# VectorE's order of two instructions in a fused attention and rational-FFN kernel: the odd unit's numerator ahead of the next unit's mask

## The chip, the cores and the metric

The kernel runs on one core of a Trainium2 chip. The metric is the device time of one execution in microseconds. A core has five engines that run their own instruction streams in order and wait for each other by semaphores: TensorE (PE, with its weight loads shown as PEld), VectorE (DVE), ScalarE (ACT), GpSimd (POOL) and SyncE (SP, which issues the DMAs here). Matmul results lie in PSUM, all else in SBUF.

## The reference

Two layers: an attention through 32 inducing points, and an FFN whose activation is a rational function. The output of the first (4 batches of 12480 tokens, 128 wide) is the input of the second (hidden width 2048).

```python
h = mab(I, x)                 # 32 inducing points look at all 12480 tokens of a batch
attn_out = mab(x, h)          # each token looks at the 32 results
h = attn_out @ w_in           # 49920 x 128 by 128 x 2048
P = a[0] + a[1] * h + a[2] * h2 + a[3] * h3
Q = 1.0 + np.abs(b[0]) * np.abs(h) + np.abs(b[1]) * h2
g = P / (Q + 1e-06)
return (g @ w_out).astype(np.float32)
```

## The kernel before

A batch has 26 blocks of 480 tokens, a block has eight **units**, and a unit is 256 of the 2048 hidden columns: two matmuls into a PSUM tile `hp` of 128 x 960. There are 832 units. The attention of the coming blocks and batches, the reshaping of weights and the output copies are cut into small **side jobs**, which `side` (line 680) puts between the units' instructions when a budget allows.

`fast_ticks` (line 777) writes the order out by hand. In tick t it emits work for units of several ages. Units come in **pairs**, an even one and the odd one behind it, which share the two halves of one SBUF tile `u`. The rational function is written as a product of factors; the denominator comes from a logarithm and a sigmoid. By the names that the profile prints, a pair passes through:

- PE `hp<-at,st`: the matmuls of `first`. `hp` has three PSUM buffers, so a unit's matmul needs what read `hp` three units earlier to be done.
- DVE `u<-hp`: the **mask** of the even unit, which clears the sign bit: u = |h|.
- ACT `u<-hp,all`: the odd unit's **magnitude** (Abs with a bias).
- POOL `l<-u,all`: the even unit's **first factor**, from the mask's u.
- DVE `l<-hp,all,l`: the **even numerator**, from h and POOL's first factor.
- DVE `l<-u,all,hp`: the **odd numerator**, from h and ACT's magnitude.
- ACT `u<-u` over both halves (128 x 1920): the **logarithm**, in place over u; it needs the last reader of u, which is the odd numerator, to be done. Then ACT `u<-u,all`: the **sigmoid**. Four pairs make a group of eight ticks: four logarithms, a change of ACT's table, four sigmoids, a change back. The group's fourth logarithm is that of its youngest pair.
- DVE `l<-l,all,u`: the even unit's **last factor**, from l and the finished u, both in SBUF; ten or eleven ticks after its start.
- POOL `u<-l,all` and `l<-u`: the same for the odd unit in two instructions (`last_on_pool`, line 827). The first overwrites the even half of u, so it waits for VectorE's last factor.
- PE `po<-l,w_out`: the matmuls of `second`, summed over the block's eight units. Then DVE `oT<-po`, the **output copy**, once in a block (that is, once in four pairs), at the start of an even tick.

In an even tick VectorE gets mask and odd numerator, and POOL the first factor. In an odd tick VectorE gets last factor and even numerator, and POOL its two instructions. Side jobs follow in each tick. Every engine keeps the program's order (`keep_in_program_order`). All recorded instructions carry line 157, that of the recording helper, so the names and shapes tell them apart.

Of the kernel before, what the change touches and what calls it, by code (L numbers as in the profile page):

```python
# [14 lines left out]
ALU = mybir.AluOpType  # L15
# [157 lines left out]
class Kernel:  # L173
# [603 lines left out]
    def fast_ticks(self, units):  # L777

        V, A, G, p = self.nc.vector, self.nc.scalar, self.nc.gpsimd, self.params
        n = len(units)
        at = lambda t: units[t] if 0 <= t < n else None
        self.first(units[0])
        for t in range(n + 13):
            u, last, d = at(t), at(t - 1), at(t - 11)
            group, turn = divmod(t - 6, 8)
            w = at(8 * group + 2 * (turn % 4))
            late = at(t - 12) and at(t - 12).key[2] == 0  # L790
            if late:
                self.fetched = self.fetch()
            if at(t - 12) and not late:
                self.second(at(t - 12))
            if at(t + 1):
                self.first(at(t + 1))
            if t % 2:
                if d:
                    V.scalar_tensor_tensor(out=d.g, in0=d.g, scalar=p.k3, in1=d.u, op0=ALU.add, op1=ALU.mult)
                    self.last_on_pool(at(t - 10), d)  # L800
                if last:
                    V.scalar_tensor_tensor(out=last.g, in0=last.h, scalar=p.k2, in1=last.g, op0=ALU.add, op1=ALU.mult)
            else:
                if u:
                    u.pair = self.mp.tile([P, 2, 2, BT], F32, tag="u", name=f"u{u.i}", bufs=7)
                    u.u = u.pair[:, 0]
                    V.tensor_scalar(out=u.u.bitcast(I32), in0=u.h.bitcast(I32), scalar1=0x7FFFFFFF, scalar2=None, op0=ALU.bitwise_and)
                if last:
                    last.g = self.new(last, "l", 14)
                    V.scalar_tensor_tensor(out=last.g, in0=last.u, scalar=p.k1, in1=last.h, op0=ALU.add, op1=ALU.mult)  # L810
                if u:
                    u.g = self.new(u, "l", 14)
                    G.tensor_scalar(out=u.g, in0=u.u, scalar1=1.0, scalar2=p.k1, op0=ALU.mult, op1=ALU.add)
            self.run_act(turn == 4)
            if w and turn < 4:
                A.activation(w.pair, w.pair, AF.Ln, bias=LAM, scale=LAM)
            elif w:
                A.activation(w.pair, w.pair, AF.Sigmoid, bias=p.lnc, scale=-2.0)
            if u and t % 2:
                u.u = last.pair[:, 1]  # L820
                A.activation(u.u, u.h, AF.Abs, bias=p.back, scale=1.0)
            self.side(u or units[-1])
            if late:
                self.second(at(t - 12))
        self.fetch()
# [123 lines left out]
```

## Time and profile before

| | us |
|---|---|
| median of 3 runs | 2594.55 (2594.13 to 2599.68) |
| profiled execution | 2594.75 |
| its span (first to last instruction) | 2592.9 |
| mean granted TensorE clock in it | 0.966 of full |

Busy time is a sum over instructions and hides waits inside an instruction: where an instruction of one kind has two typical durations, the longer one holds a wait. The columns of the group rows are: line, engine, operation, output<-inputs, shapes, count, then busy time and mean ns of one, and the idle time of the engine just before them with what ended it. The POOL and ACT groups that matter here and that are not shown further down:

```profile
L157 POOL TENSOR_TENSOR l<-u 128x960 f32<-128x960 f32 x416 | 932.2, 2241 | 34.7
L157 POOL TENSOR_SCALAR u<-l,all 128x960 f32<-128x960 f32 x416 | 445.5, 1071 | 392.8 <-DVE l L157 363.4
L157 ACT ACTIVATE u<-u 128x1920 f32<-128x1920 f32 x416 | 739.8, 1799 | 193.2 <-DVE l L157 143.0
```

There are 416 of each, one a pair.

### The profile page before, as it was taken

What the parts mean: (1) busy time and instruction counts of PE and PEld (TensorE: products, weight loads), DVE (VectorE), ACT (ScalarE), POOL (GpSimd) and SP (SyncE); (2) the same over time, 40 slices, a digit from 0 to 9 for tenths busy, and PEclk for the clock granted to TensorE, in tenths of its full rate; (3) what the DMA queues carried; (4) which work ended last, traced back from release to release, by engine and by line L of the source; (5) the groups of instructions that cost most, each with busy time, mean ns of one, the idle gap of its engine ahead of it and who ended that gap; (6) DMA issues with size and microseconds to landing.
All of it is one profiled execution on the core that took longest, in us unless ns stands there. A gap on an engine that the chain in (4) does not pass through costs nothing.

```text
span 2592.9 us, 24006 instructions
## 1 busy us (share of the span) xinstructions
PE 2249.2 (87%) x7508; PEld 1233.8 (48%) x7508; DVE 2210.1 (85%) x2318; ACT 2244.9 (87%) x1590; POOL 2011.4 (78%) x1420
## 2 busy tenths in 40 slices
PE   7798888999899789989988898888888888888887
PEld 4544444555454355544544465444435434434333
DVE  6578778899899889899898888988889888888886
ACT  1488889989889999888899998899999999999996
POOL 2267767888787788888687887887888887888887
PEclk9699989999999999999999999999999999999999
DMA  7222201211222012112321131011101001000000
GB/s 251 73 62 78 73 27 52 71 50 31 70 83 80 19 31 76 50 48 63 92 55 48 35 88 38 16 42 31 46 27 50 27 20 38 20 22 24 17 17 17
DMA packets 117357, 133.68 MB, mean 52 GB/s; under 512 B 13544, under 2 KB 115816, under 8 KB 117224
## 3 DMA queue, kind: packets, MB, share of 16 engines
q1 hardware_dynamic: 117224, 132.06, 17.6%
q8 instruction: 64, 1.05, 0.2%
q14 instruction: 69, 0.57, 0.1%
HBM read 80.89 MB, written 25.56 MB: 41 GB/s over the span
## 4 chain that ended last, share of the span: by engine, by line
DVE 32%; PE 22%; ACT 19%; POOL 18%; issue 6%; DMA 1%; SPq 1%; DVEq 0%; POOLq 0%; ACTq 0%
DVE l L157 21%; ACT u L157 13%; POOL l L157 13%; PE po L157 13%; DVE u L157 7%; ACT L157 4%; POOL u L157 4%; PE hp L157 3%; PE ph L157 2%; PE pd L157 2%; DVE oT L157 1%; POOL a L157 1%; SPq L157 1%; DVE asm L157 1%; DMA x<-x_t 1%
## 5 line engine op out<-in xcount | busy, mean ns | idle before, releaser
L157 PE MATMUL po<-l,w_out 128*128 128x480 f32 x3328 | 1545.8, 592 | 188.4 <-POOL l L157 183.6
L157 PEld LDWEIGHTS po<-l,w_out 128*128 128x128 f32 x3328 | 607.3, 194 | 773.0 <-issue 419.7
L157 POOL TENSOR_TENSOR l<-u 128x960 f32<-128x960 f32 x416 | 932.2, 2241 | 34.7
L157 ACT ACTIVATE u<-u 128x1920 f32<-128x1920 f32 x416 | 739.8, 1799 | 193.2 <-DVE l L157 143.0
L157 PE MATMUL hp<-at,st 128*128 128x480 f32 x1664 | 742.7, 529 | 98.3 <-DVE l L157 91.1
L157 ACT ACTIVATE u<-u,all 128x1920 f32<-128x1920 f32 x416 | 766.1, 1887 | 1.2
L157 POOL TENSOR_SCALAR u<-l,all 128x960 f32<-128x960 f32 x416 | 445.5, 1071 | 392.8 <-DVE l L157 363.4
L157 DVE SCALAR_TENSOR_TENSOR l<-l,all,u 128x960 f32<-128x960 f32 x416 | 597.8, 1437 | 105.7 <-ACT u L157 105.3
L157 DVE SCALAR_TENSOR_TENSOR l<-hp,all,l 128x960 f32<-128x960 f32 x416 | 503.5, 1210 | 121.8 <-POOL l L157 114.0
L157 POOL TENSOR_SCALAR l<-u,all 128x960 f32<-128x960 f32 x416 | 555.6, 1336 | 64.7 <-DVE u L157 63.7
L157 DVE TENSOR_SCALAR u<-hp 128x960 int32<-128x960 int32 x416 | 477.0, 1147 | 75.6 <-PE hp L157 74.3
L157 PEld LDWEIGHTS hp<-at,st 128*128 128x128 f32 x1664 | 312.6, 193 | 431.3 <-issue 325.3
L157 DVE SCALAR_TENSOR_TENSOR l<-u,all,hp 128x960 f32<-128x960 f32 x416 | 500.3, 1203 | 0.3 <-ACT u L157 0.3
L157 ACT ACTIVATE u<-hp,all 128x960 f32<-128x960 f32 x416 | 434.7, 1045 | 36.4 <-PE hp L157 36.3
L157 ACT ACT_TABLE_LOAD x234 | 300.2, 1283 | 4.9 <-PEq L942 0.7
L157 PE MATMUL ph<-x,eT 120*32 120x129 f32 x832 | 105.8, 280 | 9.0 <-DMA x<-x_t 6.3
L157 PEld LDWEIGHTS pd<-HT,xTb 128*120 128x120 f32 x832 | 103.3, 198 | 9.7 <-DMA xTb<-x_c 4.3
L157 PE MATMUL pd<-HT,xTb 128*120 128x32 f32 x832 | 100.5, 277 | 5.2 <-DMA xTb<-x_c 4.1
L157 PEld LDWEIGHTS ph<-x,eT 120*32 120x32 f32 x832 | 88.9, 112 | 28.0 <-issue 21.5
L157 DVE COPY oT<-po 128x480 f32<-128x480 f32 x104 | 67.3, 647 | 21.6 <-PE po L157 21.3
L157 PE MATMUL po<-at,st 128*128 128x480 f32 x104 | 80.7, 776 | 0.0
L157 PE MATMUL pc<-xTa,ind 128*128 128x480 f32 x156 | 72.2, 566 | 1.9 <-DMA xTa<-x_c 1.9
(84 smaller groups left out, 621.6 us busy)
## 6 DMA issues: line engine op xcount, KB each, us to landing
x<-x_t SPq DMA_DIRECT2D x104, 240.0 KB, 3.5
xTb<-x_c SPq DMA_DIRECT2D x104, 240.0 KB, 2.8
at<-hl SPq DMA_DIRECT2D x416, 60.0 KB, 2.0
out<-oT SPq DMA_DIRECT2D x104, 240.0 KB, 2.0
xTa<-x_c SPq DMA_DIRECT2D x78, 240.0 KB, 2.8
xTw<-x_c SPq DMA_DIRECT2D x5, 960.0 KB, 10.3
raw<-w_in SPq DMA_DIRECT2D x4, 480.0 KB, 14.2
raw<-w_out SPq DMA_DIRECT2D x5, 384.0 KB, 5.9
```

What stands on the lines that cost most here:

```text
L157: ins = call(*args, **kw)
```

## The change

In an even tick VectorE's two instructions change places: the odd numerator of the unit before comes first, then the mask of the even unit.

```diff
             else:
+                if last:
+                    last.g = self.new(last, "l", 14)
+                    V.scalar_tensor_tensor(out=last.g, in0=last.u, scalar=p.k1, in1=last.h, op0=ALU.add, op1=ALU.mult)
                 if u:
                     u.pair = self.mp.tile([P, 2, 2, BT], F32, tag="u", name=f"u{u.i}", bufs=7)
                     u.u = u.pair[:, 0]
                     V.tensor_scalar(out=u.u.bitcast(I32), in0=u.h.bitcast(I32), scalar1=0x7FFFFFFF, scalar2=None, op0=ALU.bitwise_and)
-                if last:
-                    last.g = self.new(last, "l", 14)
-                    V.scalar_tensor_tensor(out=last.g, in0=last.u, scalar=p.k1, in1=last.h, op0=ALU.add, op1=ALU.mult)
                 if u:
                     u.g = self.new(u, "l", 14)
                     G.tensor_scalar(out=u.g, in0=u.u, scalar1=1.0, scalar2=p.k1, op0=ALU.mult, op1=ALU.add)
```

VectorE's order before, in the last batch (a name such as `u3_20_6` is the tile u of batch 3, block 20, unit 6; the number behind it counts tiles):

```order
L157 TENSOR_SCALAR u3_20_6_13187<-hp3_20_6_13173 128x960
L157 SCALAR_TENSOR_TENSOR l3_20_5_13189<-u3_20_4_13161,all_193,hp3_20_5_13158 128x960
L157 SCALAR_TENSOR_TENSOR l3_19_4_13068<-l3_19_4_13068,all_193,u3_19_4_13064 128x960
L157 SCALAR_TENSOR_TENSOR l3_20_6_13191<-hp3_20_6_13173,all_193,l3_20_6_13191 128x960
L157 TENSOR_SCALAR u3_21_0_13210<-hp3_21_0_13196 128x960
L157 SCALAR_TENSOR_TENSOR l3_20_7_13212<-u3_20_6_13187,all_193,hp3_20_7_13184 128x960
```

The same place in VectorE's order after the change:

```order
L157 SCALAR_TENSOR_TENSOR l3_20_5_13187<-u3_20_4_13163,all_193,hp3_20_5_13158 128x960
L157 TENSOR_SCALAR u3_20_6_13189<-hp3_20_6_13173 128x960
L157 SCALAR_TENSOR_TENSOR l3_19_4_13068<-l3_19_4_13068,all_193,u3_19_4_13066 128x960
L157 SCALAR_TENSOR_TENSOR l3_20_6_13191<-hp3_20_6_13173,all_193,l3_20_6_13191 128x960
L157 SCALAR_TENSOR_TENSOR l3_20_7_13210<-u3_20_6_13189,all_193,hp3_20_7_13184 128x960
L157 TENSOR_SCALAR u3_21_0_13212<-hp3_21_0_13196 128x960
```

Of each pair the odd numerator (`l3_20_5`, `l3_20_7`) moved ahead of the mask (`u3_20_6`, `u3_21_0`); last factor and even numerator kept their places. The last factor now stands directly behind the mask.

ScalarE's order around the fourth logarithm of the group that ends with `u3_20_6`, after the change; it is the same before, but for the tiles' numbers:

```order
L157 ACTIVATE u3_20_4_13163<-u3_20_4_13163 128x1920
L157 ACTIVATE u3_20_6_13189<-u3_20_6_13189 128x1920
L157 ACTIVATE u3_21_0_13212<-hp3_21_1_13207,all_193 128x960
L157 ACT_TABLE_LOAD
L157 ACTIVATE u3_20_0_13115<-u3_20_0_13115,all_193 128x1920
```

The second row is the fourth logarithm, which needs the odd numerator `l3_20_7`. Nothing moved on ScalarE, TensorE, GpSimd or SyncE.

## The prediction

> **What bounds the kernel now.** I read the page's totals and its chain first.
>
> ```profile
> PE 2249.2 (87%) x7508; PEld 1233.8 (48%) x7508; DVE 2210.1 (85%) x2318; ACT 2244.9 (87%) x1590; POOL 2011.4 (78%) x1420
> DVE 32%; PE 22%; ACT 19%; POOL 18%; issue 6%; DMA 1%; SPq 1%; DVEq 0%; POOLq 0%; ACTq 0%
> ```
>
> No engine is full and the chain changes engines all the time, so the answer lies in one group of eight units (four pairs). From about 2000 us on little work stands beside the units, and groups repeat. The timelines of DVE, POOL and ACT there (start, duration, engine, operation):
>
> ```profile
> 2428.78 1.15 DVE L157 TENSOR_SCALAR u<-hp 128x960 int32<-128x960 int32 x1
> 2429.84 1.21 DVE L157 SCALAR_TENSOR_TENSOR l<-u,all,hp 128x960 f32<-128x960 f32 x1
> 2430.96 1.21 DVE L157 SCALAR_TENSOR_TENSOR l<-l,all,u 128x960 f32<-128x960 f32 x1
> 2433.06 1.22 DVE L157 SCALAR_TENSOR_TENSOR l<-hp,all,l 128x960 f32<-128x960 f32 x1 [0.89 <-POOL l L157]
> 2434.20 1.15 DVE L157 TENSOR_SCALAR u<-hp 128x960 int32<-128x960 int32 x1
> 2435.26 1.21 DVE L157 SCALAR_TENSOR_TENSOR l<-u,all,hp 128x960 f32<-128x960 f32 x1
> 2437.14 1.31 DVE L157 SCALAR_TENSOR_TENSOR l<-l,all,u 128x960 f32<-128x960 f32 x1 [0.67 <-ACT u L157]
> 2439.50 0.64 DVE L157 COPY oT<-po 128x480 f32<-128x480 f32 x1
> 2440.06 1.14 DVE L157 TENSOR_SCALAR u<-hp 128x960 int32<-128x960 int32 x1
> 2442.25 1.75 DVE L157 SCALAR_TENSOR_TENSOR l<-l,all,u 128x960 f32<-128x960 f32 x1
> 2443.93 1.20 DVE L157 SCALAR_TENSOR_TENSOR l<-hp,all,l 128x960 f32<-128x960 f32 x1
> 2451.75 1.21 DVE L157 SCALAR_TENSOR_TENSOR l<-u,all,hp 128x960 f32<-128x960 f32 x1
> ...
> 2430.96 2.07 POOL L157 TENSOR_SCALAR l<-u,all 128x960 f32<-128x960 f32 x1
> 2433.01 1.07 POOL L157 TENSOR_SCALAR u<-l,all 128x960 f32<-128x960 f32 x1
> 2434.16 2.23 POOL L157 TENSOR_TENSOR l<-u 128x960 f32<-128x960 f32 x1
> 2436.38 1.07 POOL L157 TENSOR_SCALAR l<-u,all 128x960 f32<-128x960 f32 x1
> 2441.93 1.07 POOL L157 TENSOR_SCALAR l<-u,all 128x960 f32<-128x960 f32 x1
> ...
> 2431.14 1.80 ACT L157 ACTIVATE u<-u 128x1920 f32<-128x1920 f32 x1 [1.23 <-DVE l L157]
> 2435.21 3.69 ACT L157 ACTIVATE u<-u,all 128x1920 f32<-128x1920 f32 x2
> 2453.05 1.80 ACT L157 ACTIVATE u<-u 128x1920 f32<-128x1920 f32 x1 [1.24 <-DVE l L157]
> ```
>
> Two loops are to be seen. **The ACT loop:** the group's fourth logarithm (2431.14) waits for the odd numerator (2429.84 to 2431.05). Behind it the first sigmoid ends at about 2437.1, half of the two in the row. The last factor at 2437.14 waits for it, 6.09 us after that numerator's end, and VectorE then works in order until the next fourth odd numerator (2451.75 to 2452.96). The fourth logarithms start 21.91 us apart (2431.14, 2453.05). **The POOL loop:** the even first factor and VectorE's last factor get in each other's way. At 2430.96 both start; the first factor takes 2.07 us instead of 1.07, and VectorE's even numerator waits for it until 2433.06. At 2441.93 the first factor starts 0.32 us ahead; it takes 1.07, the last factor takes 1.75 instead of 1.21, and the numerator follows it at once. Whichever starts first runs; the other stands still meanwhile.
>
> The Trainium skill ("SBUF — State Buffer", section "Who interferes with whom") says the same and more strictly: a VectorE instruction with two SBUF inputs and a GpSimd instruction that reads SBUF share a read interface, the first holds it for its whole instruction and the other fully blocks. By that rule the two in a row would need 1.21 + 1.07 us = 2.28 before the numerator starts; the row has 2.10 (2430.96 to 2433.06), so the direction agrees and the full length does not.
>
> **The change, step by step.** Nothing is added or removed; of each pair the mask and the odd numerator change places on VectorE, and the other engines keep their order.
>
> *What it gains.* The fourth logarithm is released earlier by the mask's step of 1.06 us (2428.78 to 2429.84). ACT has that much idle time in front of it (1.23), so the whole 1.06 fits into the ACT loop, once in a group. The odd numerator can also fill a wait of the mask for TensorE, and it frees its PSUM buffer earlier. It needs ACT's magnitude a step earlier; VectorE waited for nothing ahead of it, and had the mask before it as cover. That cover of 1.06 us goes; the ends are nothing and 1.06 a pair. I take nothing, since the row of the odd numerators in the stretch before (further down) shows no wait at all in 304 of them.
>
> *What it costs.* The mask, 1.12 us later (2429.84 to 2430.96, the step that now stands ahead of it), releases POOL's first factor. Until now that had the odd numerator's 1.12 us to run in. Now VectorE's last factor follows the mask at once, and POOL can't start before the mask's result is there. So the last factor is first in every pair where nothing stands between, and the first factor is held: the case of 2430.96 becomes the rule. VectorE's steps from start to start are then: even numerator 1.14 (2433.06 to 2434.20), odd numerator 1.12, mask 1.06, last factor with the wait behind it 2.10; together 5.42. POOL's steps from the last factor's start: 2.07 + 1.07 + 0.08 + 2.23, less the overlaps, end at 2436.39, so 5.43: the same, and VectorE is ready when POOL is. Where VectorE has a job or a wait of under a microsecond between mask and last factor, POOL starts first and the sum stays about the same, since the job is hidden.
>
> *The last stretch.* Four pairs of 5.42 us and one output copy (2439.50 to 2440.06, 0.56) are 22.24 us against 21.91: **+0.33 us a group**. The ACT loop no longer decides: from the odd numerator's end VectorE needs 1.12 + 1.06 + 2.10 + 1.14 + 1.12 + 1.06 us less its own 1.21, 6.39 in all, until it asks for the sigmoid that is there after 6.09. The output copies count the groups:
>
> ```profile
> L157 DVE COPY oT<-po 128x480 f32<-128x480 f32 x25 | 16.1, 643 | 0.9 <-PE po L157 0.9
> ```
>
> 25 groups between 2000 and 2550 us: +8 us.
>
> *The stretch before it,* 170 to 2000 us, by the groups of instructions, the windows and the waits:
>
> ```profile
> 170.00:2000.00 1830.00, 1628.43 (x5591) 905.92 (x5590) 1595.25 (x1592) 1641.64 (x1160) 1447.56 (x1028) 0.97 0.18 52
> L157 DVE SCALAR_TENSOR_TENSOR l<-l,all,u 128x960 f32<-128x960 f32 x303 | 434.0, 1432 | 80.6 <-ACT u L157 80.3
> L157 DVE SCALAR_TENSOR_TENSOR l<-hp,all,l 128x960 f32<-128x960 f32 x303 | 366.6, 1210 | 78.5 <-POOL l L157 70.9 <-POOL x L157 7.6
> L157 DVE SCALAR_TENSOR_TENSOR l<-u,all,hp 128x960 f32<-128x960 f32 x304 | 365.6, 1203 | 0.0
> L157 DVE TENSOR_SCALAR u<-hp 128x960 int32<-128x960 int32 x304 | 348.7, 1147 | 63.0 <-PE hp L157 61.8
> L157 DVE COPY oT<-po 128x480 f32<-128x480 f32 x76 | 49.3, 649 | 7.5 <-PE po L157 7.1
> L157 POOL TENSOR_TENSOR a<-a,asm 120x512 f32<-120x512 f32 x20 | 28.3, 1417 | 0.0
> L157 POOL TENSOR_TENSOR st<-gs,st 64x512 fp32r<-64x512 f32 x12 | 21.9, 1822 | 1.0
> DVE u L157 <- PE hp L157: 61.8, 50, 5.2
> ```
>
> 304 pairs in 1830 us are 6.02 us each now. After the change:
> - base 5.42;
> - VectorE's side jobs. Busy 1595 less the four operations' 1515, plus their overlaps of some 0.08 x 4 x 304 = 97, is 177 us, 0.58 a pair. Those ahead of the odd numerator lengthen the loop, those ahead of the last factor hide. The output copies, 0.16, are always ahead: ends 0.16 and 0.58. Taken 0.33, between them, as the other jobs lie on both sides.
> - POOL's side jobs: 28.3 + 21.9 us, 0.17 a pair, which delay the next last factor; ends 0 (beside a VectorE job) and 0.17. Taken 0.15, because the two loops are equally long and have no slack for them.
> - waits for TensorE: 61.8 us, 0.20 a pair, in 50 waits. A numerator of 1.12 can now fill each, at most 56 us: ends 0.02 and 0.20. Taken 0.09, since the longest is 5.2 and the long ones keep their rest.
> - waits for the sigmoid: 80.3 us, 0.26 a pair; ends 0 and 0.26. Taken 0.03: VectorE comes later by itself, and up to a microsecond of such a wait lets POOL's first factor go first and is not lost.
>
> Sum 6.02: **no change in this stretch**. The gain on the ACT loop and the filled waits are paid back by the even numerator's new wait. Head and tail (before 170, after 2550) have too few pairs to matter.
>
> So +8 us on the profiled execution's 2594.75, which is the median of the runs (2594.55) as near as it matters: 2603 us.
>
> **The rivals.**
> 1. *The earlier logarithm wins* (faster). POOL's jobs fall beside VectorE's and the filled waits vanish: 5.42 + 0.33 + 0.02 + 0.03 = 5.80, 0.22 less in 304 pairs, -67, +8 in the last stretch: 2536 at its end, 2536 to 2580 as a case. For it: the fourth logarithm's wait stands in nearly every group, and 61.8 us of waits can be filled. It decides from the point where less than 0.33 us of the side jobs adds up. Chance 0.25.
> 2. *POOL's first factor isn't held* after all and runs beside the last factor: VectorE's pair is 0.97 shorter, the ACT loop decides, 21.91 - 1.06 a group: 101 groups less 1.06 each, 2488. Against it: the row of 2.07. Chance 0.04.
> 3. *The order on VectorE doesn't matter*, because POOL with the last factor sets the pace before and after: 2595. For it: the two loops are equal, 5.42 and 5.43. Chance 0.07.
> 4. *All side jobs count* (slower): VectorE has no slack left, the jobs between mask and last factor don't hide (0.25 more) and the long waits stay (0.04 more): 0.29 x 304 = 88, so 2645 to 2691. Chance 0.10.
> 5. *The held one waits the whole time*: 2.28 instead of 2.10 in 403 pairs, 73 us more, 2676. Against it: the row. Chance 0.04. This is the Trainium skill's rule ("SBUF — State Buffer", "Who interferes with whom") taken to the letter.
>
> **How the numbers follow.** The forecast, VectorE bound with the even numerator waiting for POOL, has 0.50 and its own range 2588 to 2632. The range 2552 to 2655 leaves out the second rival, the far part of the first, most of the fifth and half of the fourth, about 2 in 10. A difference of 0.2% is about 5 us here, as much as a measurement of this kernel tells from none. Faster: 0.25 + 0.04 and a tail of the forecast, 0.33. Same: 0.15 of the forecast and most of the third, 0.21. Slower: the rest, 0.46.
>
> **What would show it.** The groups of instructions to compare, over the whole span:
>
> ```profile
> L157 POOL TENSOR_SCALAR l<-u,all 128x960 f32<-128x960 f32 x416 | 555.6, 1336 | 64.7 <-DVE u L157 63.7
> L157 DVE SCALAR_TENSOR_TENSOR l<-l,all,u 128x960 f32<-128x960 f32 x416 | 597.8, 1437 | 105.7 <-ACT u L157 105.3
> L157 DVE SCALAR_TENSOR_TENSOR l<-hp,all,l 128x960 f32<-128x960 f32 x416 | 503.5, 1210 | 121.8 <-POOL l L157 114.0
> L157 DVE TENSOR_SCALAR u<-hp 128x960 int32<-128x960 int32 x416 | 477.0, 1147 | 75.6 <-PE hp L157 74.3
> ```
>
> In the profile of the changed kernel POOL's `l<-u,all` should rise from a mean of 1336 ns towards 1.9 us, VectorE's `l<-l,all,u` should fall from 1437 towards 1.25, the idle time ahead of `l<-hp,all,l` should rise from 121.8 us to over 250 with POOL as releaser, ACT's wait ahead of `u<-u` for VectorE and the mask's wait for TensorE (75.6) should shrink. A group of the last stretch should take 22.2 us. I am wrong if `l<-u,all` stays near 1.1 to 1.3 us, or if the groups of the last stretch get shorter than 21.9.

## The result and the profile after

| | before | after |
|---|---|---|
| median of the runs, us | 2596.02 | 2636.49 |
| profiled span, us | 2592.9 | 2634.6 |

The changed kernel is **slower**: its time is 1.0153 of that before, with a 95% interval of 1.0135 to 1.0171, or about 40 us. (The median of before is of four runs here; the 2594.55 further up is of three of them.)

The page of the changed kernel, its totals, its chain by engine, and the groups that answer to those shown of before:

```profile
PE 2257.2 (86%) x7508; PEld 1230.0 (47%) x7508; DVE 2174.2 (83%) x2318; ACT 2250.8 (85%) x1590; POOL 2159.3 (82%) x1420
DVE 42%; POOL 26%; PE 15%; ACT 7%; issue 6%; DMA 1%; SPq 0%; DVEq 0%; POOLq 0%; ACTq 0%
...
L157 ACT ACTIVATE u<-u 128x1920 f32<-128x1920 f32 x416 | 739.5, 1799 | 174.6 <-DVE l L157 172.8
L157 POOL TENSOR_SCALAR l<-u,all 128x960 f32<-128x960 f32 x416 | 713.4, 1715 | 205.9 <-DVE u L157 190.4
...
L157 DVE SCALAR_TENSOR_TENSOR l<-hp,all,l 128x960 f32<-128x960 f32 x416 | 505.3, 1215 | 309.1 <-POOL l L157 295.5
L157 DVE SCALAR_TENSOR_TENSOR l<-l,all,u 128x960 f32<-128x960 f32 x416 | 555.1, 1335 | 44.7 <-ACT u L157 44.5
...
L157 DVE TENSOR_SCALAR u<-hp 128x960 int32<-128x960 int32 x416 | 477.9, 1149 | 26.6 <-PE hp L157 26.4
```

POOL's busy time rose by 148 us although it does the same work: its first factor grew from a mean of 1336 ns to 1715. VectorE's busy time fell by 36 us, since its last factor shrank from 1437 to 1335. The even numerator's idle time grew from 121.8 us to 309.1, nearly all of it for POOL. Two waits shrank: the mask's for TensorE from 75.6 us to 26.6, the last factor's for the sigmoid from 105.7 to 44.7. In the chain VectorE and POOL took over what ACT and TensorE lost.

By the durations in the two traces, 117 of the 416 first factors took over 1.5 us before, and 296 after. The last stretch in the timelines of DVE, POOL and ACT of the changed kernel shows why (start, duration, engine, operation):

```profile
2445.20 1.21 DVE L157 SCALAR_TENSOR_TENSOR l<-u,all,hp 128x960 f32<-128x960 f32 x1
2446.32 1.15 DVE L157 TENSOR_SCALAR u<-hp 128x960 int32<-128x960 int32 x1
2447.39 1.21 DVE L157 SCALAR_TENSOR_TENSOR l<-l,all,u 128x960 f32<-128x960 f32 x1
2449.56 1.22 DVE L157 SCALAR_TENSOR_TENSOR l<-hp,all,l 128x960 f32<-128x960 f32 x1 [0.97 <-POOL l L157]
2450.70 1.21 DVE L157 SCALAR_TENSOR_TENSOR l<-u,all,hp 128x960 f32<-128x960 f32 x1
...
2445.16 2.23 POOL L157 TENSOR_TENSOR l<-u 128x960 f32<-128x960 f32 x1
2447.57 1.96 POOL L157 TENSOR_SCALAR l<-u,all 128x960 f32<-128x960 f32 x1 [0.18 <-DVE u L157]
2449.51 1.06 POOL L157 TENSOR_SCALAR u<-l,all 128x960 f32<-128x960 f32 x1
...
2446.50 1.80 ACT L157 ACTIVATE u<-u 128x1920 f32<-128x1920 f32 x1 [1.90 <-DVE l L157]
2469.06 1.80 ACT L157 ACTIVATE u<-u 128x1920 f32<-128x1920 f32 x1 [1.89 <-DVE l L157]
```

The mask ends at 2447.47. VectorE's last factor has already started (2447.39), POOL's first factor starts at 2447.57 and takes 1.96 us, and the even numerator waits 0.97 us for it. The next odd numerator starts 5.50 us after the one before (2445.20, 2450.70). The fourth logarithms are 22.56 us apart, against 21.91 before.

### The profile page after: what moved, and what is told of

It is laid out like the page before. It is cut to its first block, busy times and chain, and to the rows that moved or that the text cites. A ratio compares the mean times of both kernels' runs of the same rounds, so it can differ in the third digit from the quotient of the medians.

```text
span 2634.6 us, 23742 instructions
## 1 busy us (share of the span) xinstructions
PE 2257.2 (86%) x7508; PEld 1230.0 (47%) x7508; DVE 2174.2 (83%) x2318; ACT 2250.8 (85%) x1590; POOL 2159.3 (82%) x1420
## 4 chain that ended last, share of the span: by engine, by line
DVE 42%; POOL 26%; PE 15%; ACT 7%; issue 6%; DMA 1%; SPq 0%; DVEq 0%; POOLq 0%; ACTq 0%
DVE l L157 26%; POOL l L157 22%; DVE u L157 11%; PE po L157 9%; ACT u L157 4%; POOL u L157 2%; DVE oT L157 2%; ACT L157 2%; PE ph L157 2%; PE pd L157 2%; PE hp L157 2%; DMA x<-x_t 1%; DVE asm L157 1%; POOL a L157 1%; DVE st L157 1%
## 5 line engine op out<-in xcount | busy, mean ns | idle before, releaser
L157 ACT ACTIVATE u<-u 128x1920 f32<-128x1920 f32 x416 | 739.5, 1799 | 174.6 <-DVE l L157 172.8
L157 POOL TENSOR_SCALAR l<-u,all 128x960 f32<-128x960 f32 x416 | 713.4, 1715 | 205.9 <-DVE u L157 190.4
L157 PE MATMUL hp<-at,st 128*128 128x480 f32 x1664 | 718.3, 514 | 91.9 <-DVE l L157 88.3
L157 DVE SCALAR_TENSOR_TENSOR l<-hp,all,l 128x960 f32<-128x960 f32 x416 | 505.3, 1215 | 309.1 <-POOL l L157 295.5
L157 DVE SCALAR_TENSOR_TENSOR l<-l,all,u 128x960 f32<-128x960 f32 x416 | 555.1, 1335 | 44.7 <-ACT u L157 44.5
L157 DVE TENSOR_SCALAR u<-hp 128x960 int32<-128x960 int32 x416 | 477.9, 1149 | 26.6 <-PE hp L157 26.4
```

The lines of the kernel that those rows point to most:

```text
L157: ins = call(*args, **kw)
```

## The experiments

Two theories were set against each other. **A:** POOL's first factor is held behind VectorE's last factor, because both have inputs in SBUF that get in each other's way; the hold outweighs what the earlier fourth logarithm gains. **B:** contention plays no part; the first factor is late because its mask is late, or each swapped pair has a flat price (the expectations use the one or the other, as the run needs it). Ratios are to the time before, measured on the same chip, with 95% intervals.

### The hold taken away: one SBUF input less

In the old order and in the new one, the last factor reads one input from SBUF and one from PSUM:

```diff
-                    V.scalar_tensor_tensor(out=d.g, in0=d.g, scalar=p.k3, in1=d.u, op0=ALU.add, op1=ALU.mult)
+                    V.scalar_tensor_tensor(out=d.g, in0=d.u, scalar=p.k3, in1=last.h if last else d.u, op0=ALU.add, op1=ALU.mult)
```

> The old order, but VectorE's last factor reads one input from SBUF (the finished u) and the other from PSUM (h of the even unit before) instead of two from SBUF. This leaves out the even unit's numerator: it multiplies by h instead, so that it is a run for times alone. Theory A (the hold comes from two SBUF inputs): the last factor falls from 1437 to about 1205 ns and POOL's first factor from 1336 to about 1075 ns, and the kernel gets faster, 2480 to 2560 us. Theory B (the first factor is late because the mask that releases it comes late, contention or not): the durations stay as they were and the time is 2580 to 2600 us.

> The same last factor with one SBUF input (the even unit's numerator left out in the same way), in the order of the change. To be compared with the run of the old order with that last factor. Theory A: without the hold the swap costs nothing, so at most 5 us slower than that run and possibly up to 60 us faster, by the earlier fourth logarithm; the even numerator's idle time stays under 120 us. Theory B: the swap still costs about 40 us.

Old order: 2506.27 us, ratio 0.9656 (0.9636 to 0.9675). New order: 2451.33 us, ratio 0.9445 (0.9427 to 0.9464). So **without the hold the swap makes the kernel 55 us faster**, where with it, it makes it 40 us slower. In the page's groups the last factors now stand under the odd numerators' names (827 together). The old order:

```profile
L157 DVE SCALAR_TENSOR_TENSOR l<-u,all,hp 128x960 f32<-128x960 f32 x827 | 977.7, 1205 | 155.3 <-ACT u L157 154.2
...
L157 ACT ACTIVATE u<-u 128x1920 f32<-128x1920 f32 x416 | 736.0, 1798 | 117.2 <-DVE l L157 63.8
...
L157 DVE TENSOR_SCALAR u<-hp 128x960 int32<-128x960 int32 x416 | 478.3, 1150 | 120.5 <-PE hp L157 114.9
...
L157 POOL TENSOR_SCALAR l<-u,all 128x960 f32<-128x960 f32 x416 | 446.3, 1073 | 83.2 <-DVE u L157 81.5
```

The new order:

```profile
L157 ACT ACTIVATE u<-u 128x1920 f32<-128x1920 f32 x416 | 733.3, 1798 | 37.3 <-DVE l L157 35.2
L157 POOL TENSOR_SCALAR l<-u,all 128x960 f32<-128x960 f32 x416 | 446.0, 1072 | 245.0 <-DVE u L157 230.2
...
L157 DVE SCALAR_TENSOR_TENSOR l<-hp,all,l 128x960 f32<-128x960 f32 x416 | 505.2, 1214 | 45.2 <-POOL l L157 26.8
L157 DVE TENSOR_SCALAR u<-hp 128x960 int32<-128x960 int32 x416 | 478.7, 1151 | 44.4 <-PE hp L157 44.4
```

POOL's first factor takes 1.07 us in both, and the last factor 1.2. In the new order the first factor does come late (POOL waits 230 us for the mask instead of 82), but that costs little: the even numerator's idle time is 45 us (27 in the old order), and the whole is faster. Theory B, as far as it blames the late mask, is out. The logarithm's idle time falls from 117 to 37 us and the mask's from 120 to 44; the runs don't separate what each of the two is worth. By the traces 52 of the 55 us lie in the 304 pairs that had stood between 170 and 2000 us before. In the last stretch a group takes 20.9 us in the old order and 20.8 in the new one, of which ACT is busy 20.7, so that there the swap has next to nothing left to gain.

### The swap in one pair of four, and in the other three

```diff
-                if last:
+                if last and t % 8 == 0:
                     last.g = ...
                     V.scalar_tensor_tensor(out=last.g, in0=last.u, ...)
                 if u:
                     V.tensor_scalar(out=u.u.bitcast(I32), ...)
+                if last and t % 8:
+                    last.g = ...
+                    V.scalar_tensor_tensor(out=last.g, in0=last.u, ...)
```

The other run has the two conditions exchanged.

> The swap in one pair of four only, the one whose odd numerator releases the group's fourth logarithm; the other three keep the old order. Theory A (POOL's first factor is held behind VectorE's last factor, so each swapped pair makes the even numerator wait about 1 us; the earlier fourth logarithm is worth something): the one swapped pair has slack towards the sigmoid, so its wait is partly free and the ACT loop is up to 1 us a group shorter: 2565 to 2600 us, a group of the last stretch 21.2 to 21.9 us. Theory B (each swapped pair costs the same, a quarter of the measured +40 us, and the earlier logarithm is worth nothing): 2606 us, a group of 22.07 us.

> The swap in the other three pairs of four, not in the one ahead of the fourth logarithm. Theory A: the cost without the gain, so as slow as the full change or slower, 2632 to 2665 us, a group of the last stretch 22.2 us or more. Theory B: three quarters of the cost, 2626 us, a group of 22.40 us.

The fourth pair alone: 2574.77 us, ratio 0.9926 (0.9907 to 0.9946). The other three: 2651.8 us, ratio 1.0219 (1.0202 to 1.0235). **The swap in the fourth pair is worth 20 us; in the other three it costs 57.** The two together give +38, about what the full change gave (+40), so the places add up. Both times are in theory A's ranges; B's 2606 and 2626 us for a flat price are outside both intervals (2570 to 2580 and 2647 to 2655 us). The page's groups of the run with the fourth pair:

```profile
L157 ACT ACTIVATE u<-u 128x1920 f32<-128x1920 f32 x416 | 738.0, 1799 | 125.3 <-DVE l L157 119.4
...
L157 POOL TENSOR_SCALAR l<-u,all 128x960 f32<-128x960 f32 x416 | 618.4, 1486 | 90.4 <-DVE u L157 89.2
...
L157 DVE SCALAR_TENSOR_TENSOR l<-hp,all,l 128x960 f32<-128x960 f32 x416 | 504.3, 1212 | 196.0 <-POOL l L157 185.4
L157 DVE SCALAR_TENSOR_TENSOR l<-l,all,u 128x960 f32<-128x960 f32 x416 | 583.5, 1403 | 43.1 <-ACT u L157 43.1
```

And of the run with the other three:

```profile
L157 ACT ACTIVATE u<-u 128x1920 f32<-128x1920 f32 x416 | 739.7, 1799 | 250.8 <-DVE l L157 190.4
...
L157 DVE SCALAR_TENSOR_TENSOR l<-hp,all,l 128x960 f32<-128x960 f32 x416 | 504.5, 1213 | 226.2 <-POOL l L157 213.8
L157 DVE SCALAR_TENSOR_TENSOR l<-l,all,u 128x960 f32<-128x960 f32 x416 | 567.6, 1365 | 111.4 <-ACT u L157 110.8
```

With the fourth alone the even numerator's idle time grows by 74 us (121.8 to 196.0), but the last factor's wait for the sigmoid falls by 63 (105.7 to 43.1), and ACT's idle ahead of the logarithm by 68 (193.2 to 125.3). With the other three the numerator's idle time grows by 104 and the sigmoid's wait stays (111.4). In the last stretch, however, the fourth alone gained nothing:

```profile
2475.00 1.80 ACT L157 ACTIVATE u<-u 128x1920 f32<-128x1920 f32 x1 [1.23 <-DVE l L157]
2496.87 1.80 ACT L157 ACTIVATE u<-u 128x1920 f32<-128x1920 f32 x1 [1.20 <-DVE l L157]
```

21.87 us a group against 21.91. There POOL's instructions and VectorE's last factor together leave hardly a gap: by the traces 0.19 us a pair is covered by neither before, and 0.17 with the fourth alone. So the ACT loop was probably not the only limit; no run here takes the two apart. Of the 20 us, 15 were gained in the 304 pairs beside side jobs (10 when the version was run again).

### A small job between mask and last factor

In the new order, a copy of 192 columns from PSUM follows the mask:

```diff
                     V.tensor_scalar(out=u.u.bitcast(I32), in0=u.h.bitcast(I32), ...)
+                    V.tensor_copy(out=self.spot, in_=u.hp[:, 0, 0:192])
```

> The changed order with one more VectorE instruction in every pair, a copy of 192 columns from PSUM between the mask and the last factor, some 0.25 us and over 100 us of added VectorE work in all. Theory A (what starts first holds the other): POOL's first factor now starts ahead of the last factor, falls from 1715 to about 1100 ns, the last factor rises from 1335 to about 1700 ns, the even numerator's idle time falls from 309 us to under 120, and the added work is nearly free: 2620 to 2655 us. Theory B (VectorE is full, and the even numerator waits only because the mask is late): the added work adds up, 2700 us or more.

2649.44 us, ratio 1.0214 (1.0198 to 1.0231): 13 us more than the changed kernel's median (16 by the ratios, which is fairer, as the chips differ) for some 110 us of added work (416 steps of 0.27 us in the rows below). The page's groups, and rows from its DVE and POOL timelines:

```profile
L157 DVE SCALAR_TENSOR_TENSOR l<-l,all,u 128x960 f32<-128x960 f32 x416 | 673.1, 1618 | 36.3 <-ACT u L157 36.2
L157 POOL TENSOR_SCALAR l<-u,all 128x960 f32<-128x960 f32 x416 | 575.0, 1382 | 164.6 <-DVE u L157 163.5
...
L157 DVE SCALAR_TENSOR_TENSOR l<-hp,all,l 128x960 f32<-128x960 f32 x416 | 503.3, 1210 | 128.4 <-POOL l L157 124.5
...
2465.98 0.35 DVE L157 COPY spot<-hp 128x192 f32<-128x192 f32 x1
2466.25 1.99 DVE L157 SCALAR_TENSOR_TENSOR l<-l,all,u 128x960 f32<-128x960 f32 x1
2471.74 1.22 DVE L157 SCALAR_TENSOR_TENSOR l<-l,all,u 128x960 f32<-128x960 f32 x1
...
2466.17 1.07 POOL L157 TENSOR_SCALAR l<-u,all 128x960 f32<-128x960 f32 x1 [0.72 <-DVE u L157]
2471.76 2.05 POOL L157 TENSOR_SCALAR l<-u,all 128x960 f32<-128x960 f32 x1
```

At 2466.17 POOL starts 0.08 us ahead of the last factor: POOL takes 1.07 us and the last factor 1.99. In the next pair the last factor is ahead by 0.02 and the roles are exchanged. Over this whole run, of the 251 pairs in which one starts up to 0.1 us before the other, the one that starts first ran unhindered in 239. In these rows the two cases alternate: where the first factor is held, POOL's chain ends later. So the first factor's mean fell to 1382 ns only, not to 1100, the last factor rose to 1618 ns, not to 1700, and the idle time fell to 128 us, not under 120. The time is in theory A's range.

### Another order: the numerator behind the last factor

Mask, last factor, odd numerator, even numerator, so that the hold is hidden under the odd numerator. (In odd ticks VectorE's part is written ahead of TensorE's, so that a PSUM buffer is not given away before its last reader.)

```diff
             if t % 2:
                 if d:
                     V.scalar_tensor_tensor(out=d.g, in0=d.g, scalar=p.k3, in1=d.u, ...)
                     self.last_on_pool(at(t - 10), d)
+                odd = at(t - 2)
+                if odd:
+                    odd.g = ...
+                    V.scalar_tensor_tensor(out=odd.g, in0=odd.u, scalar=p.k1, in1=odd.h, ...)
                 if last:
                     V.scalar_tensor_tensor(out=last.g, in0=last.h, scalar=p.k2, in1=last.g, ...)
```

In a second version the fourth pair's odd numerator stays ahead of the mask.

> Another order: mask, last factor, odd numerator, even numerator. The held first factor has the odd numerator's 1.1 us to finish in. Theory A: POOL's first factor stays long (1.8 to 2.0 us), but the even numerator hardly waits (idle under 100 us). The fourth logarithm is released about 1.1 us later than before, so the ACT loop (logarithm, sigmoid, last factor and back to the fourth odd numerator) gets 1 to 2 us a group longer: 2650 to 2780 us, a group of the last stretch 22.8 to 24 us. If the earlier or later fourth logarithm plays no part (theory B), it is faster than before, 2520 to 2580 us.

> That order in three pairs of four, and in the fourth the odd numerator ahead of the mask, so that the fourth logarithm is released early. Theory A: the even numerator waits in one pair of four only, the ACT loop is short, and what is left is POOL with the last factor, 5.3 us a pair: 2530 to 2595 us, a group of the last stretch 21.2 to 21.9 us. Theory B, in which every swapped pair costs its share: 2600 to 2620 us.

All pairs: 2870.64 us, ratio 1.1068 (1.1047 to 1.1089), slower than either theory had it. With the fourth ahead: 2609.21 us, ratio 1.0058 (1.0041 to 1.0075), above theory A's 2530 to 2595 and inside theory B's 2600 to 2620. The groups with all pairs:

```profile
L157 PE MATMUL hp<-at,st 128*128 128x480 f32 x1664 | 752.1, 536 | 405.2 <-DVE l L157 391.5
L157 ACT ACTIVATE u<-u 128x1920 f32<-128x1920 f32 x416 | 740.8, 1801 | 411.3 <-DVE l L157 389.5
...
L157 DVE SCALAR_TENSOR_TENSOR l<-l,all,u 128x960 f32<-128x960 f32 x416 | 591.2, 1421 | 395.3 <-ACT u L157 395.3
...
L157 DVE SCALAR_TENSOR_TENSOR l<-hp,all,l 128x960 f32<-128x960 f32 x416 | 503.1, 1209 | 5.5 <-POOL l L157 5.2
```

And with the fourth ahead:

```profile
L157 DVE SCALAR_TENSOR_TENSOR l<-hp,all,l 128x960 f32<-128x960 f32 x416 | 503.0, 1209 | 83.3 <-POOL l L157 79.3
...
L157 ACT ACTIVATE u<-hp,all 128x960 f32<-128x960 f32 x416 | 435.6, 1047 | 100.7 <-PE hp L157 98.6
```

The hold is hidden as expected: the even numerator waits 5.5 us in all. But the late numerator has two customers. The fourth logarithm waits 411 us, and the last factor 395 for the sigmoid: the ACT loop. And TensorE waits 391 us for VectorE before it can fill `hp` again (91.1 before), which the expectations had left out. The first factor's mean is 1605 ns, under the expected 1800 to 2000. The mean granted clock of TensorE is 0.921 in this run (0.966 before); what part of the slowdown goes with that is not shown. With the fourth ahead the logarithm's idle time is 118.5 us (193.2 before) and the last factor's wait for the sigmoid 111 (105.7 before), but TensorE still waits 127 us for VectorE before it fills `hp`, and ACT's magnitude 98.6 us for late matmuls (36.3 before). So the time fits theory B, but its reason does not: the even numerator, which should pay for each swapped pair, waits less than before the change (83.3 us against 121.8). The late `hp` is the likely cause; no run isolates it.

### A second place beside the fourth

The swap in the fourth pair and one more: the pair behind it (`t % 8 in (0, 2)`) or the one ahead of it (`t % 8 in (0, 6)`), with the fourth alone once more beside them.

> The swap in the fourth pair alone, once more, beside the two runs that add a second place. Both theories now take its measured ratio: 0.9926 of the time before, 2570 to 2582 us.

> The swap in the fourth pair and in the next one, ahead of the last factor that waits for the group's first sigmoid. Theory A (the hold costs only where the last factor follows the mask at once): where the sigmoid is later than the mask by 0.2 us or more POOL starts first, so the second swap costs little, and a wait of the mask for TensorE is filled: within 10 us of the run with the fourth alone. Theory B (every swapped pair costs about 1 us of VectorE and is repaid only by the logarithm): some 25 us slower than the fourth alone.

> The swap in the fourth pair and in the one ahead of it, where nothing waits for a sigmoid and the last factor follows the mask at once. Theory A: the hold costs in full there, and the odd numerator that it brings forward releases nothing: 10 to 40 us slower than the fourth alone. If filling the mask's waits for TensorE (25 of 101 such pairs have one) is worth more than the hold, it is as fast or faster.

The fourth alone: 2577.59 us, ratio 0.9934 (0.9916 to 0.9951). With the pair behind it: 2582.79 us, 0.9955 (0.9940 to 0.9969). With the one ahead of it: 2581.45 us, 0.9953 (0.9937 to 0.9970). Each second place is 4 to 5 us slower by the medians, but the intervals overlap, so the order of the three is not settled. The pair behind was expected within 10 us of the fourth alone, and is; the pair ahead was expected to cost 10 to 40 us and cost less.

All three are faster than both kernels. The swap in the fourth pair alone has the lowest median: **0.7% below the kernel before**, measured twice.

## Why the prediction was right, and where its size was off

- **The forecast's mechanism held.** It said that the last factor would be first wherever nothing stands between it and the mask, the first factor held, and the even numerator would wait for it. The first factor was to rise to about 1.9 us and rose to 1.72 on the mean, 1.96 in the rows of the last stretch; the last factor was to fall to 1.25 and fell to 1.34; the numerator's idle time was to pass 250 us and is 309. The runs with one SBUF input show that the hold is the cause: without it the same swap gains 55 us.
- **The size was off**, +40 us where +8 was forecast. The result lies inside the whole range, 2552 to 2655, but 2636.49 us is above 2632, the end of the forecast's own range, and slower had a chance of 0.46 only. That the whole range still holds it is in part luck: its upper part was there for the fourth and fifth rivals.
- **In the last stretch** (99 pairs) the traces have +16 us where +8 was forecast. The term that was mis-sized is the last factor with the wait behind it, taken as 2.10 us from the row at 2430.96. It measures 2.17 (2447.39 to 2449.56), so that the pair takes 5.50 instead of 5.42 and the group 22.56 instead of 22.24; 0.08 us in 99 pairs is 8 us, the whole miss there. In the row at 2430.96 both instructions began together, and the first factor ended 0.86 us after the last factor did. Behind the mask POOL begins later (0.18 us in the rows shown), and then the first factor ends about 0.93 us after it (2447.57 + 1.96 against 2447.39 + 1.21): 0.93 to 0.95 us in all 276 pairs of the changed kernel in which the last factor began first, by 0.06 to 1.21 us. The same timeline of before had such a case, with a wait of 0.97 us instead of 0.89:

```profile
2447.24 1.34 DVE L157 SCALAR_TENSOR_TENSOR l<-l,all,u 128x960 f32<-128x960 f32 x1
2449.55 1.22 DVE L157 SCALAR_TENSOR_TENSOR l<-hp,all,l 128x960 f32<-128x960 f32 x1 [0.97 <-POOL l L157]
2447.55 1.97 POOL L157 TENSOR_SCALAR l<-u,all 128x960 f32<-128x960 f32 x1
```

- **In the stretch before it** no change was forecast, and the same 304 pairs take 32 us longer in the traces (1832.8 and 1865.2 us), from 6.03 to 6.14 a pair. There it was other terms of the sum. Groups and waits of the changed kernel, 170 to 2000 us:

```profile
L157 DVE SCALAR_TENSOR_TENSOR l<-l,all,u 128x960 f32<-128x960 f32 x298 | 403.7, 1355 | 36.2 <-ACT u L157 36.1
L157 DVE SCALAR_TENSOR_TENSOR l<-hp,all,l 128x960 f32<-128x960 f32 x299 | 363.0, 1214 | 207.5 <-POOL l L157 194.0 <-POOL x L157 13.6
L157 DVE TENSOR_SCALAR u<-hp 128x960 int32<-128x960 int32 x298 | 342.3, 1149 | 19.1 <-PE hp L157 18.9
DVE l L157 <- POOL l L157: 194.0, 192, 2.0
```

  The even numerator waits for POOL in 192 pairs, not in all. The last factor with the wait behind it is 2.03 us on the mean, less than the 2.10 that was taken. Waits for the sigmoid are 0.12 us a pair where 0.03 was taken, and waits for TensorE 0.06 where 0.09 was taken. VectorE's own side jobs, with their waits, still fill 0.58 us a pair, where 0.33 was taken for them and 0.15 for POOL's. So the mis-sized terms of this stretch are the side jobs (+0.10) and the waits for the sigmoid (+0.09), and the hold gives 0.07 and TensorE 0.03 back. No run takes the side jobs apart. The pairs ahead of this stretch and the tail behind the last one are 4 and 2 us shorter after the change; the runs don't show why.
- **The gain was there** and was overpaid, as forecast. The runs show it twice: 55 us where there is no hold, 20 us where the swap stands in the fourth pair alone. But it does not come as 1.06 us in each group: in the last stretch neither gained more than 0.15 us a group. One sign was wrong: ACT's wait for VectorE ahead of the logarithm was to shrink and grew, from 143.0 to 172.8 us, while its idle time there for all reasons fell from 193.2 to 174.6. VectorE had probably become the slower of the two, so that ACT waited for it more, although each release came earlier in VectorE's own order.
- **"ACT loop no longer decides"** was right: the last factor's wait for the sigmoid fell from 105.7 to 44.7 us, and ACT fell from 19% to 7% of the chain.
- **The rivals:** the first (the logarithm wins) needed the hold to be cheap; its mechanism is real, its place was only one pair of four. The second (no hold) was wrong for this kernel and is what the one-input run shows. The third may be half right: in the last stretch POOL with the last factor left hardly a gap before, which is the likely reason why the fourth pair alone gained nothing there. The fourth is in part right: the side jobs cost about 0.10 us a pair more than was taken (it had 0.25), but the long waits for TensorE did not stay. The fifth was not needed: 2.17 is nearer to 2.10 than to its 2.28.

## What to carry to other kernels

Before two instructions change places, ask what ran in the shadow of the one that moves: here the odd numerator, with one input in SBUF, was the cover under which POOL could read SBUF undisturbed, and the swap put a two-input instruction in its place. An order that is right for one pair in four may be wrong for the other three, so an instruction that releases a slow loop should be moved only where that loop hangs on it. A step that is taken from one row should be taken from a row in which the two instructions start in the order that the change will give them.

## What the runs showed of the hardware

- The held one does not wait the whole time. POOL's first factor takes 1.07 us alone and ended 0.93 to 0.95 us after VectorE's two-input instruction in all 276 pairs of the changed kernel in which that one began first. So at least 0.12 us of its work lies inside the other's recorded time.
- The order of the starts decides who is held. Where VectorE began first, POOL's first factor took over 1.5 us in every pair: 81 of 81 before, 276 of 276 after. Where POOL was ahead by more than 0.1 us, it ran unhindered in 219 of 223 pairs before. With leads of POOL under 0.1 us the recorded starts do not settle it: with the small job between, POOL ran unhindered in 158 of 170 such pairs, in the kernel before in 6 of 36.
- Taking one SBUF input from an instruction that itself got hardly shorter (1.2 us alone in either form) made the old order 3.4% faster, and the new order 7.0% (2451.33 us against 2636.49; 5.5% below the kernel before), both times by what ran beside it.
